# Selective attention and a gated convolution unit on one core: the last batch in two token parts, Q and K transposed by row halves, free bank pairs, and a new order

## The chip, the cores and the metric

The kernel runs on one core of a Trainium2 chip. The core has TensorE (PE, matrix products and transposes), VectorE (DVE), ScalarE (ACT), GpSimd (POOL) and SyncE (SP, which here only issues transfers), and 16 DMA engines that move data between memory and the on-chip buffer. Products of TensorE land in PSUM, eight banks of 512 float32 values on each of 128 partitions. The metric is the device time of one execution in microseconds (us). The profiled execution tells the span (first to last instruction) beside its own time.

## What is computed

Attention over 8 batches, 8 heads, 576 tokens, head width 64, with a bias from a running sum, then a gated unit over the joined heads (512 wide): a causal convolution with five taps gives a gate, one matrix a value, another the output.

```python
scores = scale * np.matmul(q, k.transpose(0, 1, 3, 2))
s_pos = np.maximum(s, 0.0)
cum = np.cumsum(s_pos, axis=-1)
bias = -(cum[:, :, :, None] - cum[:, :, None, :])
scores = np.where(causal, -1000000000.0, scores + np.minimum(bias, 0.0))
attn = softmax(scores)
x = matmul(attn, v), heads joined
for k in range(5):
    gate_pre += conv_w[k][None, None, :] * xp[:, k:k + S, :]
gate = 1.0 / (1.0 + np.exp(-gate_pre))
val = x @ w_val
out = gate * val @ w_out
```

## The kernel before

The work is cut into 32 units n, each a batch b = n // 4 and a pair of heads p = n % 4. One long list of steps, `ORDER`, was written by a planner. Each entry names a step, its indices, the engine that does it (S, G, T, A, V for SyncE, GpSimd, TensorE, ScalarE, VectorE) and where its result goes: a number of a PSUM bank, or of a buffer. The entries are emitted in that order, so each engine's queue is the list cut down to its own entries, and an engine works strictly in that order; waits between engines follow from the data.

The steps of a unit, with their lines:

- Loads `ld_q`, `ld_k` (L405, L410), tails of 64 tokens `ld_t` (L433), `ld_v` (L441 to L445); all on SyncE. Casts to bf16 `c_q`, `c_k` (the helper `copy`, L348, which is also the line of every evacuation).
- `qt` (L464): transposes of Q and K of the pair against an identity, eight of 128 x 128 into one bank; `qe` copies them to `QKT`. `tt`, `te` (L454): the tails in float32.
- `s0`, `s1`, `s2` (L475): three score steps of 512 columns for each head of the pair; the two heads lie in the upper and lower 64 rows of the operands, and write two neighbouring banks. `e0`, `e1`, `e2` (L523): exponentials of 2 x 512 into `P`. `s4`, `e4` (L500): the last 64 keys, for all four pairs at once after batch 0. The causal part is masked either with two further products (L486) or, for 16 units, on GpSimd (`mk`, L529).
- `vp` (L448): V scaled by the weights of the running sum, on GpSimd or VectorE. `av0`, `av` (L540): products of `P` and V for the two heads, 15 each, with a column of ones that gives the sum; `rec` (L545) and `nm` (L549) divide.
- `xt` (L562) transposes the result, `xe` copies it to `xT`; `t1` to `t4` (L584, L586 on VectorE, L588 on GpSimd) add the taps into `gp`; a tap on GpSimd needs a product `p2` to `p4` first (L573 on ScalarE, L575 on GpSimd). `th` (L598): tanh.
- `val` (L606): the value products, two halves of 288 tokens in two neighbouring banks; `glu` (L614) multiplies both halves with the gate. `out`, `outa` (L623): output products for 128 tokens; `oe` evacuates, `st` (L631) stores.
- `wu` (L556): products that nobody reads. `chk0`, `chk` (L634 to L641), `cnt`, `cntc` (L647, L656), `flag`: a test at the end that the reciprocals and the tap ratios lie in the range for which this path holds.

A pair of banks is always two neighbours:

```python
def pair(tok):
    j = at[tok][0]
    return bank[:, j:j + 2, :]
```

The list begins and ends thus:

```
ld_q.0.0:S wu.0:T:0 ld_s:S wu.1:T:7 ld_k.0.0:S wu.2:T:0 wu.3:T:7 ld_k.0.1:S wu.4:T:0 ld_t.0:S wu.5:T:7 wu.6:T:0
...
wu.19:T:7 ld_v.0.0:S wu.20:T:2 tt.0:T:0 qt.0.0.q:T:1 qt.0.0.k:T:2 qe.0.0.q:V cwT:T:3 qe.0.0.k:A wu.21:T:7 te.0:V
...
oe.3.8:V:2 st.3.4:S out.3.5:T outa.3.7:T:3 st.3.8:S oe.3.5:V:0 out.3.7:T outa.3.6:T:0 st.3.5:S oe.3.7:V:1 out.3.6:T
cnt:T:1 st.3.7:S oe.3.6:V:3 cntc:V st.3.6:S flag:S
```

Of the kernel before, what the change touches and what calls it, by code (L numbers as in the profile page):

```python
# [18 lines left out]
NKB = 5  # L19
# [152 lines left out]
WIN = [0, 128, 256, 384, 448]  # L172
BIG, TINY, FAR = 2.0 ** 100, -2.0 ** -70, -2.0 ** 27
# [4 lines left out]
ld_q.0.0:S wu.0:T:0 ld_s:S wu.1:T:7 ld_k.0.0:S wu.2:T:0 wu.3:T:7 ld_k.0.1:S wu.4:T:0 ld_t.0:S wu.5:T:7 wu.6:T:0  # L178
wu.7:T:7 ld_cw:S c_q.0.0:G wu.8:T:0 relu:V ld_q.0.2:S wu.9:T:7 scan:V wu.10:T:0 ld_q.0.1:S wu.11:T:7 wu.12:T:0
wu.13:T:7 ld_q.0.3:S wu.14:T:0 c_k.0.1:A wu.15:T:7 c_k.0.0:V wu.16:T:0 ld_k.0.2:S wu.17:T:7 centre:V wu.18:T:0  # L180
wu.19:T:7 ld_v.0.0:S wu.20:T:2 tt.0:T:0 qt.0.0.q:T:1 qt.0.0.k:T:2 qe.0.0.q:V cwT:T:3 qe.0.0.k:A wu.21:T:7 te.0:V
wu.22:T:6 ld_k.0.3:S s0.0:T:4:0 cwc:V s1.0:T:0 ld_v.0.1:S e0.0:A decT:T:2 qt.0.1.k:T:6 c_q.0.1:V wu.23:T:7 e1.0:A
qe.0.1.k:V mk.0:G qt.0.1.q:T:3 s2.0:T:4 qe.0.1.q:V wu.24:T:6 ld_q.1.0:S:0 e2.0:A wu.25:T:7 c_k.0.2:V c_q.0.3:G
s0.1:T:0:1 c_q.0.2:V qt.0.3.q:T:3 expw:A ld_k.1.0:S:2 s4.0.0:T:4 qe.0.3.q:V qt.0.2.q:T:6 vp.0.0:G e4.0.0:A
qt.0.2.k:T:7 e0.1:A qe.0.2.q:V s1.1:T:2 s4.0.1:T:4 qe.0.2.k:V ld_k.1.1:S wu.26:T:6 e1.1:A c_k.0.3:G av0.0:T:0 s2.1:T:6
e4.0.1:A ld_q.1.1:S s0.2:T:2:0 vp.0.1:V e2.1:A av.0:T s2.2:T:4 rec.0:V e0.2:A av0.1:T:6 ld_v.0.2:S nm.0:V av.1:T
c_q.1.0:G:0 e2.2:A qt.0.3.k:T:2 rec.1:V xt.0:T:3 qe.0.3.k:V mk.2:G qt.1.0:T:0 xe.0:A nm.1:V ld_v.0.3:S s1.2:T:4
qe.1.0:A wu.27:T:1 c_k.1.0:G:1 t1.0:V:0 xt.1:T:2 s0.3:T:6:1 e1.2:A xe.1:V s4.0.3:T:0 c_k.1.1:G t2.0:V ld_t.1:S e0.3:A
s4.0.2:T:4 t1.1:V:1 p2.1:G:0 e4.0.2:A ld_v.1.2:S t3.0:V e4.0.3:A s1.3:T:6 s2.3:T:4 e1.3:A c_q.1.1:G ld_v.1.4:S
# [8 lines left out]
c_q.2:G:0 ld_t.3:S xt.4:T:7 t1.5:V:0 val.1.1:T xe.4:A val.3.0:T:2 glu.1:V p3.5:A:1 val.3.1:T t1.4:V:2 p2.5:A:0
tt.2:T:4 t3.5:G s2.7:T:0 te.2:A glu.3:V qt.2.0:T:5 e2.7:A xt.6:T:6 t3.4:V val.0.0:T:2 p4.5:G:1 val.0.1:T qe.2.0:A
t2.4:V av0.7:T:0 t4.5:G qt.2.1:T:4 th.2:A:1 glu.0:V av.7:T qe.2.1:A xe.6:V val.2.0:T:2 rec.7:V t4.4:V c_k.2:G:0  # L200
val.2.1:T p2.6:A:1 s0.9:T:4:1 nm.7:V th.4:A:2 wu.32:T:7 glu.2:V s1.9:T:0 e0.9:A cast_wo:G xt.7:T:7 t1.6:V:2 qt.2.2:T:2
e1.9:A qt.2.3:T:3 t4.6:V s1.8:T:4 qe.2.2:A s0.8:T:0:0 t2.5:G xe.7:V out.0.2:T:6 t1.7:V:1 e0.8:A out.0.3:T:2 t2.6:G
t3.7:V qe.2.3:A out.0.1:T:0 t2.7:V oe.0.3:A:0 p3.6:G:0 out.0.0:T:1 oe.0.2:A:1 st.0.3:S oe.0.1:V:2 e1.8:A val.4.0:T:2
t4.7:V t3.6:G val.4.1:T oe.0.0:A:3 s0.10:T:6:2 th.7:A:1 glu.4:V st.0.0:S s4.2.3:T:0 s2.8:T:4 mk.8:G st.0.2:S e4.2.3:A
vp.2.0:V val.6.0:T:2 ld_v.3.4:S e2.8:A val.7.0:T:0 ld_t.4:S vp.2.2:G vp.2.1:V val.6.1:T th.6:A:2 val.7.1:T e0.10:A
ld_v.3.0:S c_k.3:G:0 av0.8:T:4 glu.6:V av.8:T ld_v.3.3:S glu.7:V th.5:A:0 s2.9:T:6 ld_v.3.1:S s2.10:T:2 rec.8:V e2.9:A
val.5.0:T:0 nm.8:V ld_v.3.2:S mk.10:G val.5.1:T e2.10:A st.0.1:S av0.9:T:6 glu.5:V ld_q.5:S:4 c_q.3:G:1 av.9:T
s1.10:T:2 rec.9:V tt.3:T:0 nm.9:V e1.10:A xt.8:T:1 s0.11:T:4:1 xe.8:V vp.2.3:G te.3:A s1.11:T:6 t1.8:V:0 av0.10:T:2
e0.11:A qt.3.1:T:0 p4.8:G:0 av.10:T p3.8:A:1 qe.3.1:V qt.3.0:T:4 e1.11:A out.0.7:T:5 t4.8:G rec.10:V qe.3.0:A nm.10:V
xt.9:T:0 xe.9:V xt.10:T:2 oe.0.7:A:1 t2.8:V s1.12:T:6 p4.9:G:0 xe.10:A s0.12:T:4:2 t1.9:V:2 out.0.6:T:3 e0.12:A t3.8:G  # L210
t1.10:V:1 out.0.8:T:1 e1.12:A oe.0.6:V:3 s2.11:T:4 mk.12:G oe.0.8:A:0 t3.9:V s2.12:T:6 st.0.6:S e2.11:A out.0.4:T:3
ld_k.5:S:0 t4.10:V t4.9:G qt.3.3:T:1 th.8:A:0 oe.0.4:V:2 av0.11:T:4 ld_q.4:S:3 qe.3.3:A t2.10:V vp.3.2:G tt.4:T:3
av.11:T e2.12:A te.4:V st.0.7:S qt.3.2:T:1 st.0.8:S rec.11:V vp.3.1:G t2.9:V out.0.5:T:3 qe.3.2:A nm.11:V th.9:A:1
vp.3.3:G s0.14:T:0:1 t3.10:V s0.13:T:6:0 e0.14:A s4.3.3:T:4 oe.0.5:V:3 xt.11:T:2 c_q.5:G:0 e4.3.3:A xe.11:V s2.13:T:0
# [57 lines left out]
def main_path(ctx, tc, q, k, v, s, moe_w_val, moe_conv_w, moe_w_out, out, okcnt):  # L272
# [469 lines left out]
```

## Time and profile before

| | us |
|---|---|
| three runs | 193.15, 196.77, 196.71 (median 196.71) |
| profiled execution | 193.35 |
| its span | 191.6 |

The profile's page gives the busy time of each engine. Its views used below: the waits (who waited for whom: total, times, longest), the timeline (start, duration, engine, line, operation), the chain of waits (which work, followed back from the last instruction, set the end), the groups (busy time and mean duration of like instructions, then the engine's idle time just before them and what ended it), the windows (busy time of PE, PEld, DVE, ACT, POOL in a stretch, then the granted TensorE clock as a share of full speed, the DMA share and GB/s). A group's mean duration counts the overlap of pipelined instructions; busy time divided by their number does not.

### The profile page before, as it was taken

What the parts mean: (1) busy time and instruction counts of PE and PEld (TensorE: products, weight loads), DVE (VectorE), ACT (ScalarE), POOL (GpSimd) and SP (SyncE); (2) the same over time, 40 slices, a digit from 0 to 9 for tenths busy, and PEclk for the clock granted to TensorE, in tenths of its full rate; (3) what the DMA queues carried; (4) which work ended last, traced back from release to release, by engine and by line L of the source; (5) the groups of instructions that cost most, each with busy time, mean ns of one, the idle gap of its engine ahead of it and who ended that gap; (6) DMA issues with size and microseconds to landing.
All of it is one profiled execution on the core that took longest, in us unless ns stands there. A gap on an engine that the chain in (4) does not pass through costs nothing.

```text
span 191.6 us, 6160 instructions
## 1 busy us (share of the span) xinstructions
PE 176.6 (92%) x2481; PEld 119.3 (62%) x2481; DVE 172.9 (90%) x279; ACT 166.2 (87%) x214; POOL 166.8 (87%) x136
## 2 busy tenths in 40 slices
PE   6999796899998999999997899999999999989991
PEld 2457483578556846677755577675756764757740
DVE  5597999889989799998999999999999899999973
ACT  2179999979999699989899989999999999898930
POOL 6036989998999989999999999999999999998910
PEclk9999999699999999999999999999999999999999
DMA  5998999999999997999999999279550005200515
GB/s 149 269 258 305 255 185 288 317 335 239 238 298 292 192 260 285 307 399 189 194 192 314 363 344 216 107 249 254 139 159 29 29 5 201 76 2 3 221 74 207
DMA packets 62281, 40.43 MB, mean 211 GB/s; under 512 B 47333, under 2 KB 49381, under 8 KB 62250
## 3 DMA queue, kind: packets, MB, share of 16 engines
q1 hardware_dynamic: 62250, 40.01, 76.9%
q8 instruction: 20, 0.33, 0.7%
q14 instruction: 11, 0.09, 0.2%
HBM read 30.57 MB, written 9.44 MB: 209 GB/s over the span
## 4 chain that ended last, share of the span: by engine, by line
PE 33%; DVE 21%; ACT 21%; POOL 10%; issue 9%; DMA 3%; SPq 1%; DVEq 0%; ACTq 0%; POOLq 0%
ACT P L523 9%; PE bank L540 9%; PE bank L623 6%; POOL gp L588 5%; PE bank L475 5%; PE bank L606 5%; DVE gp L586 4%; PE bank L464 3%; DVE xn L549 3%; ACT QKT L348 3%; DVE QKT L348 3%; DVE glu L614 3%; ACT th L598 3%; DMA tail<-in_k_dram 3%; POOL pr L575 2%
## 5 line engine op out<-in xcount | busy, mean ns | idle before, releaser
L523 ACT ACTIVATE P<-bank 128x1024 bf16<-128x1024 f32 x96 | 94.5, 1039 | 4.0 <-PE bank L475 2.4
L588 POOL TENSOR_TENSOR gp<-gp,pr 128x572 f32<-128x572 f32 (+2 forms) x38 | 56.2, 1486 | 3.7 <-ACT pr L573 0.9
L586 DVE SCALAR_TENSOR_TENSOR gp<-bank,cwr,gp 128x574 f32<-128x574 bf16 (+2 forms) x58 | 46.1, 802 | 0.6
L475 PE MATMUL bank<-QKT 64*128 64x128 bf16 (+4 forms) x576 | 38.0, 241 | 5.1 <-ACT P L523 2.8
L606 PE MATMUL bank<-xT,wv 128*128 128x288 bf16 x256 | 36.1, 286 | 2.1 <-DVE xT L348 0.6
L540 PE MATMUL bank<-Vp,P 128*128 128x65 bf16 x960 | 35.9, 194 | 0.7 <-ACT P L523 0.5
L540 PEld LDWEIGHTS <-P 128*128 128x128 bf16 x960 | 33.4, 98 | 4.6 <-issue 2.5
L623 PE MATMUL bank<-wo,glu 128*128 128x512 bf16 x144 | 35.3, 380 | 0.1
L575 POOL TENSOR_TENSOR pr<-xT,cwr 128x572 f32<-128x572 bf16 (+2 forms) x28 | 32.7, 1175 | 1.4 <-DVE xT L348 0.8
L475 PEld LDWEIGHTS <-QKT 64*128 64x128 bf16 x576 | 18.5, 94 | 21.8 <-issue 14.8
L606 PEld LDWEIGHTS <-wv 128*128 128x128 bf16 x256 | 23.8, 97 | 10.7 <-issue 3.4
L448 POOL TENSOR_TENSOR Vp<-vst,w 128x650 bf16<-128x650 f32 x22 | 29.0, 1335 | 0.5 <-ACT w L369 0.5
L598 ACT ACTIVATE th<-gp,cwr 128x576 f32<-128x576 f32 (+1 forms) x33 | 25.2, 780 | 3.1 <-POOL gp L588 1.9
L584 DVE SCALAR_TENSOR_TENSOR gp<-xT,cwr,bank 128x576 f32<-128x576 bf16 x32 | 25.7, 809 | 1.3 <-ACT xT L348 0.2
L549 DVE TENSOR_TENSOR xn<-bank,recs 128x640 bf16<-128x640 f32 x32 | 26.0, 819 | 0.6
L348 ACT COPY QKT<-bank 128x1024 bf16<-128x1024 bf16 (+1 forms) x25 | 24.9, 1014 | 1.8 <-PE bank L464 1.8
L614 DVE SCALAR_TENSOR_TENSOR glu<-th,bank 128x576 bf16<-128x576 f32 (+1 forms) x33 | 23.9, 731 | 2.5 <-ACT th L598 1.1
L529 POOL TENSOR_SCALAR_AFFINE_SELECT P<-P 128x1024 bf16<-128x1024 bf16 x16 | 17.5, 1094 | 8.8 <-ACT P L523 8.8
L623 PEld LDWEIGHTS <-glu 128*128 128x128 bf16 x144 | 12.5, 97 | 14.0 <-issue 2.3
L464 PE MATMUL bank<-ident,qkb 128*128 128x128 bf16 x256 | 19.3, 219 | 0.3 <-DVE gp L586 0.3
L464 PEld LDWEIGHTS <-qkb 128*128 128x128 bf16 x256 | 15.4, 98 | 3.5 <-issue 1.6
L348 POOL CAST qkb<-first 128x2048 bf16<-128x2048 f32 (+2 forms) x11 | 15.5, 1410 | 0.8 <-DMA first<-in_k_dram 0.4
(61 smaller groups left out, 182.7 us busy)
## 6 DMA issues: line engine op xcount, KB each, us to landing
out_dram<-ot SPq DMA_DIRECT2D x36, 256.0 KB, 3.1
vst<-in_v_dram SPq DMA_DIRECT2D x28, 256.0 KB, 5.8
first<-in_q_dram SPq DMA_DIRECT2D x7, 512.0 KB, 7.3
first<-in_k_dram SPq DMA_DIRECT2D x7, 512.0 KB, 8.2
qkf<-in_q_dram SPq DMA_DIRECT2D x5, 512.0 KB, 6.2
qkf<-in_k_dram SPq DMA_DIRECT2D x5, 512.0 KB, 6.5
vst<-in_v_dram SPq DMA_DIRECT2D x15, 128.0 KB, 4.6
first<-in_q_dram SPq DMA_DIRECT2D x6, 256.0 KB, 4.6
```

The source lines that it names most:

```text
L348: (act.copy if e is act else e.tensor_copy)(dst, src)
L464: pe.transpose(bank16[:, at["qt", b, p, *w][0], c * 512 + j * 128:c * 512 + (j + 1) * 128], qk_src(which, b, p, j if w else 4 * c + j), ident)
L475: pe.matmul(ps[:, hh, c0:c0 + nq], QKTs[b % 2][r, 1, p, k0:k0 + 128], QKTs[b % 2][r, 0, p, q0:q0 + nq], **kw)
L523: act.activation(out=Pt(n)[:, :, step * 512:(step + 1) * 512], in_=pair((f"s{step}", n)), func=AF.Exp, scale=0.125)
L540: pe.matmul(ps[:, qb * 65:qb * 65 + 65], lhsT, Vps[b % 2][:, kb, 2 * p + hh, :], start=(kb == 0), stop=(kb == qb))
L549: vec.tensor_tensor(xns[b % 2][:, :, p * 128:(p + 1) * 128].rearrange("t g (w d) -> t w g d", w=2), pair(("av", n))[:, :, 0:325].rearrange ...
L575: pool.tensor_tensor(pr, xTs[b % 2][:, c, 4:4 + S - m], r.to_broadcast([128, S - m]), ALU.mult)
L586: vec.scalar_tensor_tensor(gp[:, m:S], xps(n)[:, 0:S - m], r, gp[:, m:S], ALU.mult, ALU.add)
L588: pool.tensor_tensor(gp[:, m:S], gp[:, m:S], prs[at[f"p{m}", n][0]][:, m:S], ALU.add)
L598: act.activation(out=thof(n)[:, r], in_=gps[at["t1", n][0]].rearrange("p (h s) -> p h s", h=2)[:, r], func=AF.Tanh, scale=cwr[:, n % 4, 4:5])
L606: pe.matmul(ps, wv[:, dc, c * 128:(c + 1) * 128], xTs[b % 2][:, dc, 4 + o:4 + o + 288], start=(dc == 0), stop=(dc == 3))
L623: pe.matmul(bank_of(u, i), glu2[:, c, i * 128:i * 128 + 128], wo[:, c, :], start=(c == 0), stop=(c == 3))
```

## The change

- The units of the last batch (28 to 31) run in two token parts of 384 and 192 tokens. Their three score steps and exponentials of 2 x 512 become four of 2 x 384 (`u0` to `u3`, `f0` to `f3`), the mask has two steps (`mk`, `ml`), and `av`, `rec`, `nm`, `xt`, `xe`, the taps, their products, `th`, `val` and `glu` each come once for a part.
- From batch 1 on, the transposes of Q and K of two pairs are one step `qq`: each 128 x 128 transpose becomes two, of the upper and lower 64 rows, into two banks; `qe` reads both banks.
- A pair of banks may be any two.
- `glu` runs once for each half of the value products, everywhere, and each half has a bank of its own.
- The test at the end takes a minimum and a sum of the reciprocals instead of two compares for each.
- `ORDER` is new. In it six of batch 0's loads are issued by ScalarE; the casts of batch 1's Q and batch 2's K are on ScalarE; all 32 `vp` are on GpSimd (22 before); ScalarE has 28 output evacuations and VectorE 8 (20 and 16 before); GpSimd masks 15 whole units and four parts of units 28, 30 and 31 (16 whole units before); there are 40 unread products (33 before), eleven of them together behind unit 5's second score step (`s1.5`); two output blocks rather than five are held back for the last tanh; the last batch's parts are interleaved.

```diff
+HALF_STEPS = [
+    [(0, 0, 128, 0), (1, 128, 128, 128), (2, 256, 128, 256)],
+    [(0, 128, 256, 0), (1, 256, 128, 256)],
+    [(3, 384, 128, 0), (3, 512, 64, 128), (0, 384, 192, 192)],
+    [(1, 384, 192, 0), (2, 384, 192, 192)],
+]
+PARTS = [(0, 384, (0, 1, 2)), (384, 576, (3, 4))]
...
+ld_k.0.0:A ld_q.0.0:S ld_k.0.1:A wu.0:T:0 ld_t.0:S wu.1:T:7 wu.2:T:0 wu.3:T:7 ld_q.0.1:S wu.4:T:0 ld_k.0.2:A ld_s:S
+wu.5:T:7 ld_q.0.2:A wu.6:T:0 ld_v.0.0:S ld_k.0.3:A wu.7:T:7 c_k.0.0:V ld_q.0.3:A qt.0.0.k:T:0 wu.8:T:2 c_q.0.0:V
+qe.0.0.k:A qt.0.0.q:T:1 ld_v.0.1:S wu.9:T:7 c_k.0.1:V qe.0.0.q:A wu.10:T:2 qt.0.1.k:T:0 s0.0:T:1+2:0 qe.0.1.k:V
+wu.11:T:7 e0.0:A tt.0:T:3 ld_k.1.0:S:2 wu.12:T:0 te.0:V wu.13:T:7 wu.14:T:0 c_q.0.1:G wu.15:T:7 s2.0:T:3+1 ld_k.1.1:S
...
+t4.31.1:G glu.29.1:V out.3.5:T:0 st.3.6:S th.30.1:A:1 glu.28.1:V st.3.4:S t2.31.1:V glu.30.1:V val.31.1:T:7
+th.31.1:A:2 outa.3.8:T:2 oe.3.5:A:2 glu.31.1:V chk:V out.3.8:T st.3.5:S outa.3.7:T:0 oe.3.8:A:3 out.3.7:T st.3.8:S
+cnt:T:2 oe.3.7:A:1 cntc:V st.3.7:S flag:S
...
+        if ("qq", b, p // 2) in at:
+            copy(e, QKTs[b % 2][:, :, p, 0:512].rearrange("d w (r x j) -> d w r x j", r=2, j=8),
+                 both_rows(b, p).rearrange("d r (j x w) -> d w r x j", w=2, j=8))
+            return
...
-    def pair(tok):
-        j = at[tok][0]
-        return bank[:, j:j + 2, :]
+    def both(two):
+        lo, hi = two
+        return bank[:, lo:hi + 1:hi - lo, :]
...
+    def half_T(out, src, r):
+        return pe.transpose(out, src[64 * r:64 * r + 64, :], ident[64 * r:64 * r + 64, 64 * r:64 * r + 64])
+
+    def both_rows(b, p):
+        lo, hi = sorted(at["qq", b, p // 2])
+        return bank16[:, lo:hi + 1:hi - lo, p % 2 * 512:p % 2 * 512 + 512]
+
+    def qk_T2(e, b, h):
+        for p in range(2):
+            for j in range(8):
+                for r in range(2):
+                    half_T(both_rows(b, 2 * h + p)[:, r, j * 64:j * 64 + 64], qk_src(None, b, 2 * h + p, j), r)
...
-    def within(e, o, rf):
-        e.tensor_scalar(o, rf, 5e-35, None, ALU.is_ge)
-        e.scalar_tensor_tensor(o, rf, 1.5e31, o, ALU.is_le, ALU.mult)
+    def extremes(e, i, rf):
+        e.tensor_reduce(stat[:, i:i + 1], rf, AX.X, ALU.min)
+        e.tensor_reduce(stat[:, 2 + i:3 + i], rf, AX.X, ALU.add)
```

More of the change, by code (lines that the diff above doesn't have):

```diff
@@ L198 @@
[L198 to L202, printed above, removed]
@@ L329, in main_path @@
     cw = ots[3][0:5]
-    cwT = one.tile([128, 4, 5], FP32, name="cwT")
     cwr = one.tile([128, 4, 5], FP32, name="cwr")
@@ L404, in f @@
             if b == 0:
-                sync.dma_start(out=first[part][which],
+                e.dma_start(out=first[part][which],
                                in_=(q, k)[which][0, HP[part], 0:512, :].rearrange("h (p j) d -> p h (j d)", j=4))
@@ L565, in x_evac @@
+    def both_rows(b, p):
[4 more added lines that the diff above has]
+            for j in range(8):
+                for r in range(2):
+                    half_T(both_rows(b, 2 * h + p)[:, r, j * 64:j * 64 + 64], qk_src(None, b, 2 * h + p, j), r)
+    def x_evac(e, n, *h):
         b, p = divmod(n, 4)
-        copy(e, xTs[b % 2][:, p, 4:4 + S], xps(n))
+        lo, hi = span(*h)
+        copy(e, xTs[b % 2][:, p, 4 + lo:4 + hi], xps(n, *h)[:, lo:hi])
@@ L594, in tanh @@
     def tanh(e, n, *hf):
+        if split(n):
+            lo, hi = span(*hf)
+            act.activation(out=ths[at["th", n, *hf][0]][:, lo:hi], in_=gps[at["t1", n, *hf][0]][:, lo:hi],
+                           func=AF.Tanh, scale=cwr[:, n % 4, 4:5])
+            return
         if hf:
```

405 lines of the change are left out of this document (236 added, 169 removed).

## The prediction

> **What bounds the kernel now.** I read the page first, then ScalarE's waits, then its start and its end.
>
> ```profile
> span 191.6 us, 6160 instructions
> ...
> PE 176.6 (92%) x2481; PEld 119.3 (62%) x2481; DVE 172.9 (90%) x279; ACT 166.2 (87%) x214; POOL 166.8 (87%) x136
> ```
>
> Four engines are within 11 us of each other, so none alone is the bound: a gain needs a shorter start, a shorter end, fewer waits, or less work on all four. The change moves work onto ScalarE, so I balance that engine's time. Who kept it waiting:
>
> ```profile
> ACT qkb L348 <- DMA first<-in_k_dram: 5.4, 1, 5.4
> ACT P L523 <- PE bank L475: 2.4, 3, 1.6
> ACT th L598 <- POOL gp L588: 1.9, 4, 0.7
> ACT QKT L348 <- PE bank L464: 1.8, 1, 1.8
> ACT ot L348 <- PE bank L623: 1.5, 3, 0.7
> ACT P L523 <- PE bank L486: 1.1, 2, 1.0
> ACT th L598 <- DVE ok L634: 1.0, 1, 1.0
> ```
>
> Its start in the timeline, and the chain of waits there:
>
> ```profile
> 0.82 1.28 ACT L348 ACT_TABLE_LOAD   x1 [0.82 <-PEq L726]
> 7.54 0.62 ACT L348 CAST qkb<-first 128x512 bf16<-128x512 f32 x1 [5.44 <-DMA first<-in_k_dram]
> 9.97 0.59 ACT L348 COPY QKT<-bank 128x512 bf16<-128x512 bf16 x1 [1.81 <-PE bank L464]
> 11.18 1.02 ACT L523 ACTIVATE P<-bank 128x1024 bf16<-128x1024 f32 x1 [0.62 <-PE bank L475]
> ```
> ```profile
> 0.82 0.46 SPq L405
> ...
> 3.76 4.96 DMA tail<-in_k_dram
> ...
> 8.86 0.63 PE bank L454 x4
> ```
>
> The first exponential starts at 11.18, because TensorE's queue has the tails' transposes (L454) ahead of the first Q, K transposes, and the tail lands at 8.7. The end (ScalarE, chain, VectorE):
>
> ```profile
> 182.88 0.96 ACT L598 ACTIVATE th<-gp,cwr 128x288 f32<-128x288 f32 x2 [0.96 <-DVE ok L634]
> ```
> ```profile
> 182.77 4.62 PE bank L623 x20
> ```
> ```profile
> 187.46 0.69 DVE L348 COPY ot<-bank 128x512 f32<-128x512 f32 x1 [0.23 <-PE bank L623]
> ```
>
> After the last tanh (183.84) come 7.76 us in which five output blocks are made one after another. From the first exponential to that point are 172.66 us, of which ScalarE works 166.2 less 1.28, 0.62, 0.59 (before) and 0.6 (one evacuation after) = 163.1, and idles 9.5. So the span is 11.2 + 163.1 + 9.5 + 7.8 = 191.6, and the profiled run took 193.35, 1.75 more. Of the runs one stands there (193.15); the median, 196.71, is 3.4 higher. I forecast a run like the profiled one.
>
> **Work on ScalarE.** Rows (engine, busy, mean):
>
> ```profile
> L523 ACT ACTIVATE P<-bank 128x1024 bf16<-128x1024 f32 x96 | 94.5, 1039 | 4.0 <-PE bank L475 2.4 <-PE bank L486 1.1
> ...
> L348 ACT COPY QKT<-bank 128x1024 bf16<-128x1024 bf16 x24 | 24.3, 1031 | 0.0
> L598 ACT ACTIVATE th<-gp,cwr 128x576 f32<-128x576 f32 x31 | 24.3, 796 | 2.1 <-POOL gp L588 1.9 <-DVE glu L614 0.2
> ...
> L348 ACT COPY ot<-bank 128x512 f32<-128x512 f32 x20 | 12.0, 606 | 1.5 <-PE bank L623 1.5
> ...
> L348 ACT COPY xT<-bank 128x576 bf16<-128x576 bf16 x11 | 7.1, 650 | 0.6 <-PE bank L562 0.5
> ...
> L500 ACT ACTIVATE P<-bank 128x512 bf16<-128x512 f32 x7 | 4.4, 627 | 0.0
> ...
> L573 ACT ACTIVATE pr<-bank,cwr 128x573 f32<-128x573 bf16 x5 | 3.7, 744 | 0.1
> ```
>
> Busy per instruction: exponential 0.98 at 1,024 wide, 0.63 at 512, so 0.81 at 768. The last batch's 12 become 16 of 768: 16 x 0.81 - 12 x 0.98 = +1.1. Tanh: 0.78 whole, 0.48 at half, so about 0.61 and 0.45 for 384 and 192 tokens; 28 + 4 pairs against 31 + 2 halves: +1.0. Output evacuations 20 to 28: +4.8. Casts: two of 1,024 (1.0 each, as the QKT copy) and one of 2,048 (1.7, on the same slope) for the one of 0.62: +3.1. QKT copies: one whole less (-1.0), two of 512 more (+1.2). X evacuations: six whole fewer, six parts at about 0.4: -1.4. Tap products: two whole fewer, one part: -1.1. Sum +7.7. Two evacuations follow the last tanh rather than one, so 163.1 + 7.7 - 0.6 = **170.2** lie before it.
>
> **The other engines.**
>
> ```profile
> L448 POOL TENSOR_TENSOR Vp<-vst,w 128x650 bf16<-128x650 f32 x22 | 29.0, 1335 | 0.5 <-ACT w L369 0.5
> ...
> L614 DVE SCALAR_TENSOR_TENSOR glu<-th,bank 128x576 bf16<-128x576 f32 x31 | 23.0, 749 | 2.1 <-ACT th L598 0.8 <-PE bank L606 0.5 <-ACT ot L348 0.4
> ...
> L448 DVE TENSOR_TENSOR Vp<-vst,w 128x650 bf16<-128x650 f32 x10 | 12.2, 1232 | 0.0
> L556 PE MATMUL bank<-ident 128*128 128x512 bf16 x33 | 12.0, 492 | 1.6 <-POOL ident masks.py:199 1.4 <-DVE QKT L348 0.2
> ...
> L348 DVE COPY ot<-bank 128x512 f32<-128x512 f32 x16 | 11.0, 686 | 1.2 <-PE bank L623 1.1
> ...
> L614 DVE SCALAR_TENSOR_TENSOR glu<-th,bank 128x288 bf16<-128x288 f32 x2 | 0.9, 454 | 0.3 <-ACT th L598 0.3
> ```
> ```profile
> L588 POOL TENSOR_TENSOR gp<-gp,pr 128x572 f32<-128x572 f32 (+2 forms) x38 | 56.2, 1486 | 3.7 <-ACT pr L573 0.9 <-DVE recs L545 0.9 <-DVE gp L586 0.3
> ```
>
> VectorE: value products by halves make 64 of 0.45 from 31 of 0.74 and two halves, +4.9; ten V scalings go, -12.2; eight output evacuations go, -5.5. Whole taps go from 90 to 84 and 18 parts come, priced like the gate's wholes and halves of the same shape: 18 x 0.45 - 6 x 0.74 = +3.7; parts of normalising and the rest about +3. Sum -6. GpSimd: ten V scalings at 1.32 come, +13.2; its additions go from 38 wholes to 28 and 10 parts of about 0.8, -14.9 + 8; products likewise some -3; masks and casts -0.8. Sum +2.5. The scalings stand in its queue ahead of masks and taps, and the tanh that waits for the taps (1.9 above) can wait longer. Both stay below ScalarE, which becomes the longest.
>
> A copy out of two banks at once is new for Q, K. I price it as before, since the exponentials read two banks at 0.98 for 1,024 elements, no more than the copy of 1,024 from one bank (24.3/24 = 1.01); if it cost a tenth more, ScalarE would have 2.4 more. The bank pair that an exponential reads need no longer be neighbours: the same price, and the same doubt with it.
>
> TensorE: 224 whole transposes become 448 of half the rows and half the width. Whole ones and the nearest row of 64 wide products from half the rows:
>
> ```profile
> 89.91 1.51 PE L464 MATMUL bank<-ident,qkb 128*128 128x128 bf16 x24
> ```
> ```profile
> 151.10 0.29 PE L475 MATMUL bank<-QKT 64*128 64x64 bf16 x8
> ```
>
> A whole one takes (1.51 - 0.22)/23 = 0.056, a 64 wide one (0.29 - 0.19)/7 = 0.014, since the two row halves run at once. So two pairs cost 32 x 0.014 = 0.45 instead of 16 x 0.056 = 0.90; times 14, -6.3, or nothing if the halves run in turn (32 x 0.027 is about 0.9). I take -5 for the turns between shapes. Seven more unread products at 0.36 add 2.5. Here the Trainium skill speaks against the change: TensorE: Matmul & The Clock Gate (Wait — 56ns, not 53.3ns?) says that products never start less than about 25 ns apart, which would leave 0.8 of 0.9. The row above, at 14 ns, disagrees for products from different row halves. The page TensorEngine Tiling (Array Packing), Key Properties, adds that a change of tiling mode drains the array; no row shows a price for it.
>
> **Start.** K of pair 0 is now the first load on ScalarE's queue, beside Q on SP's, and the tails' transposes come after the first scores. Loads into this tile:
>
> ```profile
> DMA to landing us min/median/max: 3.0/5.0/9.2
> ```
>
> Issued at 0.8 plus 3.0 to 5.0 (the table load may go first and take 1.3 of it): landed at 3.8 to 5.8, say 4.5. Then a cast 0.6, transposes 0.4, two evacuations of 0.6, scores 0.7: the first exponential at about **7.5** (6.8 to 8.8). The tail comes behind two or three loads, some 8 plus transpose, evacuation and scores: 9.8, so the second exponential waits 1.4. ScalarE's six issues, some 0.46 to 0.6 each, lie in the time in which it waited 5.4 for data; SP's queue loses them, so the V loads behind them are issued earlier, and all loads share what was a transfer of about 5 us each: if the first two come no sooner for it (5.0 rather than 3.0), the first exponential stands at 8.8 and 1.3 is lost.
>
> **End.** Only two blocks hang on the last tanh: gate product 0.45, five products at 4.62/20 (1.2), evacuation 0.6, store and close as before (191.6 - 188.15 = 3.45): **5.7**. The shorter closing test takes the 0.96 before the last tanh away.
>
> **Waits.** TensorE ran at half clock and ScalarE waited for it:
>
> ```profile
> 35.00:36.00 1.00, 1.00 (x6) 0.13 (x4) 1.00 (x2) 1.00 (x2) 1.00 (x2) 0.50 1.06 397
> ```
> ```profile
> 39.49 1.02 ACT L523 ACTIVATE P<-bank 128x1024 bf16<-128x1024 f32 x1 [0.96 <-PE bank L486]
> ```
>
> The unread products now stand just there, so of the 9.5 this 0.96 goes, and the closing test's 0.96. Waits for TensorE's products (1.8 + 0.9 + 0.1) I halve, as TensorE gets shorter, GpSimd's 1.9 and the other 2.9 too, since all three now run ahead of ScalarE: 1.4 + 0.95 + 1.45, and 1.4 for the tail: **5.2** (1.4 to 9.0). Any two banks making a pair costs nothing itself; it can only shift these waits.
>
> Sum: 7.5 + 170.2 + 5.2 + 5.7 + 1.75 = **190.4** (1.5% under 193.35; 3.2% under the median).
>
> **Rivals.** *ScalarE is kept full* (0.27): three engines with slack and free choice of banks leave only the tail's 1.4: 186.6. For it: the last batch's parts feed ScalarE to the end. Against: before, no engine did better than 95% in its dense stretch.
>
> *The halves don't overlap* (0.15): TensorE, with its unread products, gets longer and none of the waits on it or its followers falls: 9.0, so 194.2. For it: no transposes by halves in this trace; against: the 0.014 above.
>
> *ScalarE blocked by loads* (0.16): batch 1's Q casts and batch 2's K cast now stand in ScalarE's queue, ahead of all its exponentials of that batch; behind them wait the scores' banks, so TensorE too. By my count it reaches the first at 26, when those loads, issued at about 20, land (25 to 29). A landing of 9.2 instead of 5.0 at both places costs 8.4: 198.8. It decides from 3 us in all. Against: after the start no engine waited for a load.
>
> The forecast's case has 0.42, its own range 188 to 192.5. Range 185.5 to 196. About 2% is what a measurement can tell from no change: faster than 189.5 are the first rival and half of the forecast's case, 0.48; slower than 197.2 most of the last, 0.13; 0.39 between.
>
> **What would show it.** First exponential at 7 to 8 and a gap before the second; ScalarE busy about 174, VectorE 167, GpSimd 169; 32 half transposes of a step in some 0.65; clock 1.00 throughout; 5.7 us behind the last tanh. It is wrong if ScalarE's idle time between is outside 1.4 to 9, or if its casts wait for loads.

## The result, and the profile after

| | before | after |
|---|---|---|
| runs, us | 193.15, 193.51, 196.71, 196.77 (median 195.11) | 312.90, 314.60, 314.82, 319.55 (median 314.71) |
| ratio to before, 95% interval | 1 | 1.626 (1.615 to 1.637) |
| profiled execution and its span, us | 193.35, 191.6 | 319.55, 317.7 |
| mean granted TensorE clock in it | 0.989 | 0.822 |

The change made the kernel 63% slower. Medians take all runs, ratios only those in a kernel's faster state, and the profiled execution of after is a slower one (319.55). The page after, its head and the row of the clock:

```profile
span 317.7 us, 6693 instructions
...
PE 220.1 (69%) x2716; PEld 136.6 (43%) x2734; DVE 167.7 (53%) x320; ACT 181.0 (57%) x231; POOL 165.9 (52%) x148
...
PEclk9779675699699975657995999977699855997699
```

The work is near what was forecast for VectorE (167) and GpSimd (169), and 7 us more than forecast for ScalarE (174); no engine is busy for more than 69% of the span. So the time went into waiting, on all engines and from one end to the other. TensorE now stands idle again and again, and its granted clock is below 1 in most slices. Who waited for whom (total, times, longest):

```profile
PE bank L518 <- ACT P L569: 18.1, 24, 1.2
...
ACT P L569 <- DVE xn L626: 12.6, 9, 1.7
DVE recs L620 <- ACT P L569: 12.0, 7, 3.0
DVE gp L684 <- ACT P L569: 11.0, 6, 3.9
ACT P L569 <- PE bank L518: 10.8, 14, 1.6
ACT P L569 <- PE bank L607: 10.7, 7, 2.8
```

Three of these rows name two instructions of which neither hands data to the other. An exponential (L569) reads scores and writes `P`; the normalising step (L626) reads a product of `P` and V and writes `xn`. Nothing goes straight from the one into the other, and yet exponentials wait for it, 12.6 us in all; the reciprocals (L620) and the taps on VectorE (L684) wait for exponentials. In the waits before, none of the three pairs of lines stands at all.

One place shows how it works. The list there reads, with banks behind the engine's letter:

```
av0.4:T:3+6 av.4:T rec.4:V e0.5:A vp.1.3:G av0.6:T:0+2 nm.4:V av.6:T e1.5:A s2.5:T:1+5 rec.6:V vp.1.1:G xt.4:T:3 nm.6:V e2.5:A
```

`e0.5`, `e1.5` and `e2.5` read banks 1 and 5, 4 and 7, 1 and 5; `nm.4` reads 3 and 6, `nm.6` reads 0 and 2. The timeline of after, ScalarE and then VectorE:

```profile
63.71 1.02 ACT L569 ACTIVATE P<-bank 128x1024 bf16<-128x1024 f32 x1 [3.50 <-DVE recs L620]
65.68 1.02 ACT L569 ACTIVATE P<-bank 128x1024 bf16<-128x1024 f32 x1 [0.95 <-DVE xn L626]
68.27 1.02 ACT L569 ACTIVATE P<-bank 128x1024 bf16<-128x1024 f32 x1 [1.56 <-DVE xn L626]
```
```profile
64.76 0.82 DVE L626 TENSOR_TENSOR xn<-bank,recs 128x640 bf16<-128x640 f32 x1 [1.15 <-ACT P L569]
67.10 0.22 DVE L620 RECIPROCAL recs<-bank 128x10 f32<-128x10 f32 x1 [1.51 <-PE bank L518]
67.35 0.82 DVE L626 TENSOR_TENSOR xn<-bank,recs 128x640 bf16<-128x640 f32 x1
```

The two engines take turns: `nm.4` starts when `e0.5` ends (63.71 + 1.02 = 64.73), `e1.5` when `nm.4` ends (64.76 + 0.82 = 65.58), `e2.5` when `nm.6` ends (68.17). The banks say why. Bank 6 of `nm.4` lies between 4 and 7, bank 2 of `nm.6` between 1 and 5, and bank 3 of `nm.4` between 1 and 5. Each instruction that takes two distant banks waits as if it took all the banks between them too.

The start and the end of after, by the same view of ScalarE:

```profile
13.76 1.02 ACT L569 ACTIVATE P<-bank 128x1024 bf16<-128x1024 f32 x1 [5.09 <-PE bank L531]
...
311.46 0.46 ACT L698 ACTIVATE th<-gp,cwr 128x192 f32<-128x192 f32 x1 [0.68 <-DVE gp L684]
```

The first exponential ran at 7.65, as forecast. The second, at 13.76, reads banks 1 and 3, and its row names a product of another step (L531) in bank 2. Little of the 5.09 is due to that. The scores that it reads began only at 13.16, since TensorE had first waited 2.50 for the tail:

```profile
13.16 0.53 PE L518 MATMUL bank<-QKT 64*128 64x320 bf16 x6
```

In the run e1 below, which has no distant pairs, the same scores begin at 10.96 and the exponential 0.44 later; here it is 0.60. Behind the last tanh (311.92) stand 5.8 us, where 5.7 were forecast.

### The profile page after: what moved, and what is told of

Same layout as the page of the kernel before. It is cut to its first block, busy times and chain, and to the rows that moved or that the text cites. A ratio compares the mean times of both kernels' runs of the same rounds, so it can differ in the third digit from the quotient of the medians.

```text
span 317.7 us, 6693 instructions
## 1 busy us (share of the span) xinstructions
PE 220.1 (69%) x2716; PEld 136.6 (43%) x2734; DVE 167.7 (53%) x320; ACT 181.0 (57%) x231; POOL 165.9 (52%) x148
## 4 chain that ended last, share of the span: by engine, by line
PE 42%; ACT 28%; DVE 15%; issue 7%; POOL 4%; DMA 3%; SPq 0%; ACTq 0%; DVEq 0%; POOLq 0%
ACT P L569 17%; PE bank L717 9%; PE bank L607 9%; PE bank L518 8%; DVE xn L626 6%; ACT QKT L374 6%; PE bank L737 6%; PE bank L633 3%; ACT P L583 3%; DMA tail<-in_k_dram 3%; PE bank L639 3%; PE bank L642 2%; POOL qkb L374 2%; DVE QKT L374 2%; DVE gp L679 2%
## 5 line engine op out<-in xcount | busy, mean ns | idle before, releaser
L569 ACT ACTIVATE P<-bank 128x1024 bf16<-128x1024 f32 x84 | 84.5, 1023 | 80.8 <-DVE xn L626 12.6
L687 POOL TENSOR_TENSOR gp<-gp,pr 128x572 f32<-128x572 f32 (+6 forms) x38 | 47.3, 1247 | 58.5 <-DVE gp L684 28.3
L684 DVE SCALAR_TENSOR_TENSOR gp<-bank,cwr,gp 128x574 f32<-128x574 bf16 (+5 forms) x70 | 50.9, 739 | 18.8 <-ACT P L569 11.0
L717 PE MATMUL bank<-xT,wv 128*128 128x288 bf16 (+2 forms) x256 | 46.4, 324 | 13.6 <-ACT P L569 7.8
L607 PEld LDWEIGHTS <-P 128*128 128x128 bf16 x960 | 40.2, 108 | 22.4 <-issue 17.1
L668 POOL TENSOR_TENSOR pr<-xT,cwr 128x572 f32<-128x572 bf16 (+6 forms) x29 | 29.1, 1008 | 30.0 <-DVE xT L374 26.5
L592 POOL TENSOR_SCALAR_AFFINE_SELECT P<-P 128x1024 bf16<-128x1024 bf16 (+2 forms) x19 | 20.0, 1054 | 35.8 <-ACT P L569 32.0
L726 DVE SCALAR_TENSOR_TENSOR glu<-th,bank 128x288 bf16<-128x288 f32 (+2 forms) x64 | 27.4, 446 | 18.8 <-PE bank L717 5.5
L626 DVE TENSOR_TENSOR xn<-bank,recs 128x640 bf16<-128x640 f32 (+2 forms) x36 | 26.8, 746 | 18.0 <-ACT P L569 4.6
L679 DVE SCALAR_TENSOR_TENSOR gp<-xT,cwr,bank 128x576 f32<-128x576 bf16 (+2 forms) x36 | 26.6, 742 | 9.2 <-ACT P L569 7.3
L620 DVE RECIPROCAL recs<-bank 128x10 f32<-128x10 f32 (+2 forms) x36 | 7.5, 210 | 40.1 <-ACT P L569 12.0
L639 PE MATMUL bank<-ident,xn 128*128 128x128 bf16 x164 | 18.4, 253 | 9.5 <-DVE xn L626 4.5
L704 ACT ACTIVATE th<-gp,cwr 128x576 f32<-128x576 f32 x28 | 21.3, 772 | 0.0
```

What stands on the lines that cost most here:

```text
L569: act.activation(out=Pt(n)[:, :, step * 512:(step + 1) * 512], in_=pair((f"s{step}", n)), func=AF.Exp, scale=0.125)
L607: pe.matmul(ps[:, o:o + 65], lhsT, Vps[b % 2][:, kb, 2 * p + w, :], start=(kb == 0), stop=(kb == qb))
L626: vec.tensor_tensor(xns[b % 2][:, g, p * 128:(p + 1) * 128].rearrange("t g (w d) -> t w g d", w=2), ps[:, :, :, 0:64], recs[:, n, :, g].un ...
L668: pool.tensor_tensor(pr, xTs[b % 2][:, c, 4 + lo - m:4 + hi - m], r.to_broadcast([128, hi - lo]), ALU.mult)
L679: vec.scalar_tensor_tensor(gp[:, lo:hi], xT[:, 3 + lo:3 + hi], r, xps(n, *h)[:, lo:hi], ALU.mult, ALU.add)
L684: vec.scalar_tensor_tensor(gp[:, lo:hi], xps(n, *h)[:, lo - m:hi - m], r, gp[:, lo:hi], ALU.mult, ALU.add)
```

## The experiments

The first theory (A) is the one just read from the trace: the new line `bank[:, lo:hi + 1:hi - lo, :]` touches two banks, but the layer that records the instructions and puts in the waits takes it for the whole range from `lo` to `hi`. Waits would then follow not from the data alone, as the part on the kernel before has it, but from all the banks that an instruction is taken to touch. In after's list 153 steps have a pair of banks; in 128 the two aren't neighbours, and 337 banks lie in between. In the programs as built, a wait can be held against the banks and buffers of its two instructions: among TensorE, VectorE and ScalarE, 10 of 695 waits before join instructions that share none (all ten are those of a weight load, whose product does share one), and 355 of 759 after. The rivals of e1 to e3 put the cause elsewhere in the change.

Medians stand beside those of before on the same chip, since chips differ (193.1 to 195.5 for before):

| run | time, us | before, us | ratio (95%) | busy PE, DVE, ACT, POOL, us | clock |
|---|---|---|---|---|---|
| e1 neighbours | 200.99 | 195.03 | 1.029 (1.017 to 1.040) | 177.1, 164.4, 172.4, 165.2 | 0.972 |
| e2 before, far pairs | 378.11 | 195.03 | one run | 248.6, 178.5, 177.3, 164.1 | 0.740 |
| e3 renumbered | 255.58 | 195.03 | one run | 194.5, 165.4, 177.8, 165.7 | 0.916 |
| e4 e1 without 11 unread products | 199.75 | 195.53 | 1.025 (1.016 to 1.034) | 172.8, 164.8, 172.3, 165.3 | 0.972 |
| e5 e1 with whole transposes | 199.24 | 195.53 | 1.019 (1.007 to 1.032) | 176.4, 164.6, 172.6, 165.4 | 0.991 |
| e6 e1, first loads on SyncE | 199.26 | 195.53 | 1.019 (1.009 to 1.029) | 176.6, 164.2, 172.3, 164.0 | 0.966 |
| e7 before, value by halves | 194.37 | 195.53 | 0.994 (0.988 to 1.000) | 176.3, 175.0, 166.8, 166.5 | 0.991 |
| e8 e5, 8 evacuations on VectorE | 200.07 | 193.13 | 1.037 (1.031 to 1.043) | 180.4, 167.7, 169.2, 165.5 | 0.967 |
| e9 before, early start | 193.63 | 193.13 | 1.003 (0.999 to 1.007) | 174.8, 172.7, 166.5, 167.0 | 0.991 |
| e10 before, short test | 192.70 | 193.13 | one run | 173.7, 173.3, 166.5, 166.0 | 0.997 |
| e11 e5, e6, e8 together | 199.29 | 193.13 | 1.033 (1.026 to 1.039) | 177.7, 167.8, 169.3, 164.2 | 0.981 |
| e12 before, row halves | 209.22 | 194.79 | 1.080 (1.073 to 1.087) | 178.3, 176.1, 168.4, 167.2 | 0.973 |
| e13 before, e12's banks | 204.13 | 194.79 | 1.056 (1.050 to 1.061) | 177.3, 176.7, 168.3, 166.8 | 1.000 |

**e1: neighbours only.** After, with its order and its engines, but every pair of banks dealt anew as two neighbours; single banks are dealt anew with them:

```diff
-av0.4:T:3+6 av0.6:T:0+2 s2.5:T:1+5
+av0.4:T:6+7 av0.6:T:4+5 s2.5:T:0+1
```

> The changed kernel with every step in its place; only the bank numbers are dealt anew, so that each pair is two neighbours again. Theory A (an instruction that touches banks a and b also waits for whoever uses the banks between them): the waits between ScalarE, VectorE and TensorE on banks that they do not share are gone, ScalarE idles 5 to 10 us between its first exponential and the last tanh, 187 to 195 us. Rival B (the new order itself keeps the engines waiting): 300 us or more. Rival C (TensorE falls to half clock from the turns between whole and half transposes): 300 us or more, with the half transposes slow.

Measured: 200.99. Of the 120 us that after lost, 114 are gone (314.71 to 200.99), though on other chips. The rivals, which left the time near after's, are out; A's own range, 187 to 195, was too low by 6, and its 5 to 10 us of idle time by 7 (17.1). The place shown above, in e1's timeline:

```profile
46.67 2.85 ACT L569 ACTIVATE P<-bank 128x1024 bf16<-128x1024 f32 x3 [2.97 <-PE bank L607]
```
```profile
46.97 0.82 DVE L626 TENSOR_TENSOR xn<-bank,recs 128x640 bf16<-128x640 f32 x1
47.71 0.21 DVE L620 RECIPROCAL recs<-bank 128x10 f32<-128x10 f32 x1
47.95 0.82 DVE L626 TENSOR_TENSOR xn<-bank,recs 128x640 bf16<-128x640 f32 x1
```

The three exponentials now run in one block of 2.85 us, and VectorE normalises beside them; in after they took from 63.71 to 69.29. In e1's waits no exponential waits for `xn`.

**e2: the same fault put into before.** Before, with its own order, engines and work. The bank numbers are renamed so that each of its 171 pairs lies four banks apart:

```diff
+        if e == "T" and slots:
+            slots[0] = slots[0] // 2 + 4 * (slots[0] % 2)
-        return bank[:, j:j + 2, :]
+        return bank[:, j:j + 5:4, :]
```

> The kernel before with its plan untouched; only banks are renumbered so that the two banks of each pair lie four apart (0 and 4, 1 and 5, ...). Theory A: some 480 waits on banks in between, where the changed kernel has some 355, so 270 to 360 us, with ScalarE and VectorE waiting for each other. Rivals B and C: 193 to 197 us, since order and transposes are those of before.

Measured: 378.11, nearly twice before, past A's 360, with nothing of the change in it but the distant pairs. The foreign wait comes with them:

```profile
ACT P L523 <- DVE xn L549: 24.6, 13, 3.8
```

**e3: fewer banks between.** After, with only the names of its eight banks permuted (0, 1, ..., 7 become 0, 4, 1, 7, 2, 5, 6, 3). Which step shares which bank with which stays as it was; 83 pairs remain distant, with 188 banks between them instead of 337.

> The changed kernel with its plan and its pairs untouched; the eight banks are renumbered (0,4,1,7,2,5,6,3) so that fewer lie between two of a pair: 188 instead of 337 in all. Theory A: some 200 waits on banks in between instead of 355, so about 260 us (225 to 290). Rivals B and C: 310 to 320 us, since nothing else differs.

Measured: 255.58, where A said about 260. A permutation of names changes nothing but what lies between, so time follows that: 337 in between 315, 188 some 256, none (e1, where the numbers are dealt anew) 201. The waits by program fall in step: 355, 199 and 6 that share no bank or buffer (482 of 712 in e2). A is settled.

What is open after e1 is smaller: 2 to 3% above before, where the forecast was 2 to 3% below. The next runs take the other terms of the sum one at a time.

**e4: without the unread products.** e1 without the eleven behind `s1.5` (`wu.29` to `wu.39` left out of the list).

> e1_neighbours without its eleven unread products wu.29 to wu.39 that stand together behind s1.5. Theory A1 (what e1 lacks against the forecast is partly TensorE's queue: the eleven, 4.28 us at 41.40 in e1's timeline, hold the value products of unit 4, for which VectorE then waits 5.9 and ScalarE about 3): 196.5 to 199 us beside e1's 201, the waits of VectorE's reciprocals for the bank of the value products at 42 to 48 shrink from 5.9 to under 3. Rival (TensorE would stand there anyway, waiting for the V scalings of batch 1 that GpSimd ends only at about 46): 200 to 202, the wait moves to the V scalings. Second rival (the unread products keep the clock up, as they are meant to): above 202, with a lower granted clock behind 41 us.

Measured: 199.75, 0.3% nearer to before than e1, within the intervals, and between the range of A1 and that of the first rival. VectorE's wait at that place, in e1 and in e4, fell from 5.90 to 4.67, not to under 3:

```profile
46.71 0.22 DVE L620 RECIPROCAL recs<-bank 128x10 f32<-128x10 f32 x1 [5.90 <-PE bank L607]
```
```profile
44.45 0.22 DVE L619 RECIPROCAL recs<-bank 128x10 f32<-128x10 f32 x1 [4.67 <-PE bank L606]
```

The 60 products of `P` and V that follow, in e1 and in e4:

```profile
41.40 4.28 PE L633 MATMUL bank<-ident 128*128 128x512 bf16 x11
...
45.51 1.99 PE L607 MATMUL bank<-Vp,P 128*128 128x65 bf16 x60
```
```profile
42.54 3.46 PE L606 MATMUL bank<-Vp,P 128*128 128x65 bf16 x60 [1.72 <-ACT P L568]
```

Without the eleven, these products start 2.97 us earlier (TensorE then waits 1.72 for an exponential) and take 1.47 longer, at a lower clock (0.69 in the 10 us from 40, where e1 has 0.75). So both A1 and the second rival are half right in the mechanism, and neither in the time: the unread products take TensorE's time and the products behind them are faster for it, which gives back about half (1.47 of 2.97).

**e5: whole transposes.** e1 with each `qq` undone into two `qt` of eight 128 x 128 transposes, one bank each.

> e1_neighbours with the row halves undone: each qq becomes two qt steps of eight whole 128 x 128 transposes, one bank each. By the prediction's term (-5 us of TensorE's time for the halves): TensorE's busy time goes from e1's 177 to 181 to 184, and the time, since TensorE is again the longest engine by 8, from 201 to 202.5 to 205. Rival (the halves run one after the other, or their turns of shape cost what they save): TensorE's busy time within 1.5 of e1's, the time within 2 of it.

Measured: 199.24, not above e1's 200.99, so the price expected is not there; the rival's numbers hold (busy 176.4 against 177.1). Yet the transposes themselves are as much shorter as forecast. One step of e1 (two pairs) and the same of e5:

```profile
56.12 0.64 PE L642 MATMUL bank<-ident,qkb 64*128 64x64 bf16 x32
```
```profile
49.92 1.07 PE L504 MATMUL bank<-ident,qkb 128*128 128x128 bf16 x16
```

14 x (1.07 - 0.64) = 6.0 us. The row of e1 gives (0.64 - 0.19)/31 = 0.0145 us from one half transpose to the next, 0.19 being the duration of one alone. The Trainium skill, TensorE: Matmul & The Clock Gate (Wait — 56ns, not 53.3ns?), has 25 ns as the least; the trace disagrees for products from two row halves. What of the 6.0 was given back the rows show in part: e1 ran at a clock of 0.90 from 10 to 60 us, e5 at 1.00, and its eleven unread products took 4.28 where e5's took 2.90 (1.66 and 1.24).

**e6: who issues the first loads.** e1 with all of batch 0's first loads issued by SyncE (six `:A` become `:S`).

> e1_neighbours with all of batch 0's first loads issued by SyncE, in the order of the list. Theory A2 (the early start is bounded by what the DMA engines move, not by which engine issues): the first exponential moves from 8.04 by less than 1 us, the time is 200 to 202. Rival, the prediction's own step (the issue on ScalarE's idle queue brings the first exponential forward, since SyncE's issues take about 0.5 to 0.6 each): the first exponential at 9.5 to 11, the time 202 to 204.

Measured: 199.26; the first two exponentials:

```profile
7.81 1.02 ACT L569 ACTIVATE P<-bank 128x1024 bf16<-128x1024 f32 x1 [1.74 <-PE bank L518]
9.86 1.02 ACT L569 ACTIVATE P<-bank 128x1024 bf16<-128x1024 f32 x1 [1.02 <-PE bank L518]
```

The first is where e1 had it (8.04), the second 1.54 earlier (11.40 in e1), since TensorE starts on the tail at 7.94 rather than 9.48. The rival expected 9.5 to 11 for the first, and 202 to 204; A2's 200 to 202 is just missed. The early start comes from the order of the loads, not from a second engine that issues them. The Trainium skill says the same in DMA: Bandwidth & Descriptors (Issuing engines are not separate DMA queues): transfers of all issuing engines share the same 16 DMA engines, and a second issuer saves only the time of issuing. The trace agrees (7.81 with one issuer, 8.04 with two).

**e7: value products by halves in before.** 64 half `glu` for the 31 whole and two halves.

> Before with its 31 whole products of value and gate each done as two halves, as after has it, nothing else changed. The prediction's price: VectorE +4.9 us busy (172.9 to 177.8). VectorE is within 7 us of the longest engine: if its work is nowhere on the path that sets the end, 194 to 196 (before 195); if it is all on it, 199 to 200. Theory: in between, 196 to 198.

Measured: 194.37, within 1% of before: the case in which the work is nowhere on the path. The theory, 196 to 198, misses. VectorE's busy time rose by 2.1 (172.9 to 175.0), not 4.9; the 64 halves are busy for 25.7 us, 0.40 each, where the prediction took 0.45 from two of them.

**e8: ScalarE's added work given back.** e5 with eight output evacuations on VectorE (`oe.1.0:A:2` becomes `oe.1.0:V:2`, and so on).

> e5_whole_transposes with eight of ScalarE's output evacuations (oe.0.5, oe.1.0, oe.1.2, oe.1.6, oe.1.7, oe.1.8, oe.2.0, oe.2.1) on VectorE, at the same places of the order, as many as before had there. ScalarE's busy time falls by about 4.8 (172.6 to 168), VectorE's rises by 5.5 (164.6 to 170). Theory (what the neighbour pairs leave over before is mostly work moved onto ScalarE, which is on the path): 196 to 198 beside e5's 199.2. Rival (the engines wait for one another in this order, whoever has the work): 198.5 to 201.

Measured: 200.07; ScalarE's busy time fell by 3.4, and the time didn't. The theory falls, the rival holds: in this order, less work on ScalarE did not make the time shorter.

**e9: the early start alone.** Before with `ld_k.0.0` second and the tails behind the first scores:

```diff
-... tt.0:T:0 qt.0.0.q:T:1 qt.0.0.k:T:2 ... te.0:V ... s0.0:T:4:0 ... e0.0:A
+... qt.0.0.q:T:1 qt.0.0.k:T:2 ... s0.0:T:4:0 ... e0.0:A ... tt.0:T:0 ... te.0:V
```

> Before with its first steps in another order: K of pair 0 is the second load on SyncE's queue, the first Q, K transposes, scores and exponential stand ahead of the tails' transposes, as in after; nothing else changed. First exponential at 7 to 8 instead of 11.2 in both cases. Prediction's step (what the first exponential comes earlier, less a wait of 1.4 for the tail, is kept to the end): 192 to 193.5 beside before's 195.5. Rival, theory A2 (the loads of the next pairs land no sooner, so ScalarE waits for them and has done by 22 us what it had done before): 194.5 to 196.

Measured: 193.63 beside 193.13. ScalarE in e9, and one row of before:

```profile
7.65 1.02 ACT L523 ACTIVATE P<-bank 128x1024 bf16<-128x1024 f32 x1 [1.21 <-PE bank L475]
...
11.04 1.02 ACT L523 ACTIVATE P<-bank 128x1024 bf16<-128x1024 f32 x1 [1.85 <-PE bank L475]
...
16.53 2.85 ACT L523 ACTIVATE P<-bank 128x1024 bf16<-128x1024 f32 x3
```
```profile
17.00 2.85 ACT L523 ACTIVATE P<-bank 128x1024 bf16<-128x1024 f32 x3
```

The first exponential is 3.53 earlier (11.18 before), the sixth to eighth only 0.47, and at the end (spans 191.8 and 191.6) nothing is left. The ratio, 1.003, is where the rival had it (194.5 to 196 beside 195.5), but not quite for its reason. The second exponential reads scores that need the tail, and the tail's transposes (L454) start at 8.95, no earlier than before (8.86). ScalarE had one exponential early and then waited for the tail; behind it the steps of the next pairs follow in TensorE's queue.

**e10: the shorter closing test alone.** Before with `within` replaced by `extremes`.

> Before with the test at the end done with a minimum and a sum, as after has it. Prediction's step (the wait of 0.96 before the last tanh was for the test on VectorE): that wait goes. Rival (it was for the last tap on GpSimd, which ended at 181.45 + 1.40 = 182.85 in before's trace, 0.03 before the tanh began; the row named the engine wrongly): 0.8 to 1.1 stays. The time within 1 us of before in both cases.

Measured in the trace: the wait stays, and its row now has another name. The last tanh in e10, and the last tap of before:

```profile
182.14 0.96 ACT L599 ACTIVATE th<-gp,cwr 128x288 f32<-128x288 f32 x2 [0.95 <-POOL gp L589]
```
```profile
181.45 1.40 POOL L588 TENSOR_TENSOR gp<-gp,pr 128x573 f32<-128x573 f32 x1 [0.33 <-DVE gp L586]
```

In before the tap ended at 182.85 and the tanh began at 182.88; the test's first step (L634) ended at 182.63 + 0.26 = 182.89, no sooner, and yet the row gave its name to the wait.

**e11: the parts together.** e5 with e6's loads and e8's evacuations.

> After's plan with neighbour pairs, whole transposes, the eight evacuations on VectorE, and all first loads on SyncE (e5, e6 and e8 together). Theory: the parts add up, 195 to 198, at best even with before. Rival (each part only moves a wait): 198.5 to 201.

Measured: 199.29, 3.3% above before: the rival. Parts that moved nothing alone moved nothing together. No version with after's list beats before.

**e12 and e13: row halves alone, and their banks.** Before with `qk_T` and `qk_evac` by row halves from batch 1 on, into two neighbouring banks; the bank numbers of the list dealt anew (e12). The same numbers with whole transposes, the second bank left empty (e13).

```diff
+        if not w:
+            for j in range(8):
+                for r in range(2):
+                    half_T(both_rows(b, p)[:, r, j * 64:j * 64 + 64], qk_src(None, b, p, j), r)
+            return
```

> Before with one part of the change alone: from batch 1 on the transposes of Q and K are done by row halves, into two neighbouring banks, one pair at a time; the bank numbers of the list are dealt anew for it, nothing else changed. Prediction's term: TensorE's busy time -5 us (176.6 to about 171.5) at a full clock, and since TensorE is the longest engine by 4, the time falls by 2 to 4 beside e13. Rival (TensorE waits for the others at those places, so shorter transposes only lengthen its waits, and its clock falls with its load): TensorE's busy time falls by less than 3, the time within 1 us of e13's.

> Control for e12: before with whole transposes, but with the bank numbers of e12, which leave a second bank empty at each transpose. Theory: the dealing alone costs 0 to 2 us, so 193 to 197 beside before's 193 to 196. Rival (bank dealing sets the waits of these kernels, and is what e1 lacks against the forecast): 197 or more.

Measured: 209.22 and 204.13. In e13 its rival holds (197 or more): its fastest run, 202.41, is above the slowest of before there, 198.20. In e12 neither time holds, since it is 5 us above e13, but the rival was right that TensorE's busy time would not fall. The groups of transposes, e12 and e13 (busy, mean ns, then idle before them):

```profile
L462 PE MATMUL bank<-ident,qkb 64*128 64x64 bf16 x448 | 11.9, 192 | 5.0 <-ACT P L539 3.3 <-DVE QKT L348 0.7 <-DVE xn L565 0.7
...
L476 PE MATMUL bank<-ident,qkb 128*128 128x128 bf16 x32 | 2.8, 220 | 0.0
```
```profile
L464 PE MATMUL bank<-ident,qkb 128*128 128x128 bf16 x256 | 19.6, 219 | 2.5 <-ACT P L523 1.9 <-DVE xn L549 0.3 <-ACT QKT L348 0.2
```

The group is shorter by 19.6 - 11.9 - 2.8 = 4.9 us, the term that the prediction had. TensorE's busy time is not (178.3 against 177.3, at a clock of 0.973 against 1.000), it stands idle 2.5 us more ahead of its transposes, which now need two free banks at once, and the time is 5 us longer; what makes up the other half of the 5 is not shown. And e13 has the work, the order and the neighbours of before; only the numbers of its banks differ, and it is 5.6% slower, with TensorE idle for 200.7 - 177.3 = 23.4 us of the span (before 191.6 - 176.6 = 15.0). No bank lies between here: all that new numbers change is which earlier step must have left a bank before the next one writes it.

## Why the prediction was wrong

**The step that failed** is the last sentence of its part on waits: "Any two banks making a pair costs nothing itself; it can only shift these waits." It costs the waits of all the banks in between. The access itself is no dearer (an exponential takes 1,023 ns on average in after and 1,039 before); the waiting is. By the balance of the prediction, after's ScalarE starts its exponentials at 7.65, ends its last tanh at 311.92, and works some 177 us in between (181.0 less the table load, two copies before and three after); so it idles about 127 us, where the forecast had 5.2 and no more than 9.0. The miss is made of 127 - 5 in waits, and of 7 of work more than forecast, since instructions of ScalarE that run one at a time don't overlap with their neighbours (three exponentials in a block take 2.85, alone 3 x 1.02). Of the 122 in waits, 110 go when the pairs are neighbours (e1 idles 17.1); the other 12 are the matter of the next part. The diff had the cause in sight: a slice with a step, and a list in which 128 of 153 pairs are distant. No rival asked what the recording layer makes of a slice with a step.

**Without those waits (e1)** the sum can be checked term by term. First exponential 8.04 (forecast 7.5), work between 168.3 (170.2), idle 17.1 (5.2), end 5.85 (5.7): 199.3, and 201.08 with what lies around the span. Work and end were nearly right, the idle time was short by 12. Two of its terms are shown to be wrong, one bought nothing where it was tried, and one wait was left out:

- The early start was expected to be kept but for a wait of 1.4 us for the tail. That wait was 2.33 in e1, and e9 keeps none of 3.53.
- The closing test's 0.96 was a misnamed wait for GpSimd's tap (e10).
- TensorE's 5 us were in the transposes (4.9 in e12, 6.0 in e5) but not in its busy time, and not in the time. Waits for its products, to be halved, grew instead. ScalarE's waits in e1 (before had 2.4 in the row that answers to the first):

```profile
ACT P L569 <- PE bank L518: 6.9, 8, 2.3
...
ACT P L569 <- PE bank L607: 3.6, 3, 3.0
```

- The new step `qq` puts two pairs into the same two banks, each in its own half of them. In five of the 14 steps the two copies out of the banks (`qe`) are on different engines, and there one waits for the other, though neither needs the other's values: 3.8 us in e1 on ScalarE, where before and e5 have no such row. Without it (e5) the time is within e1's interval.

```profile
ACT QKT L374 <- DVE QKT L374: 3.8, 4, 1.4
```

Where e1 falls behind is seen in the windows from 10 to 60 us, of e1 and of before (busy time of PE, PEld, DVE, ACT, POOL, then the clock):

```profile
10.00:60.00 50.00, 42.07 (x674) 27.00 (x674) 37.96 (x66) 40.96 (x51) 39.84 (x32) 0.90 1.01 255
```
```profile
10.00:60.00 50.00, 46.24 (x711) 32.15 (x710) 46.23 (x72) 47.50 (x64) 43.39 (x34) 0.97 1.06 270
```

ScalarE does 6.5 us less in that stretch, VectorE 8.3 less. Which wait starts it, the order or the new dealing of banks, stays open: e13 shows that a dealing alone can cost more than the 3% in question, and e4, e5, e6, e8 and e11 each moved e1 by no more than its interval.

**The rest.** The price of halves for value and gate was too high (2.1 for 4.9, e7). No cast waited for a later batch's loads, so that rival did not come about. A clock of 1.00 throughout was wrong for after (0.822) and, from 10 to 60 us, for e1. The mode-change drain that the prediction cited has no row of its own in any run.

## What to carry to other kernels

Before an access with a step through banks or tiles is priced at nothing, ask what the recording layer takes it to touch: if it takes the range, each instruction waits for strangers, and in a kernel whose engines are all near full such waits multiply. A wait between two instructions that share no data is the sign of it, and a list with the names of the banks permuted is a cheap test. A bank's number is a resource of its own: here, shorter work that needs two free banks at once made the kernel 5 us slower, and a start that ran ahead of its data gained nothing.

## What the runs showed of the hardware that was not expected

- The clock was lower where TensorE stood idle for longer, and the same work then kept it busy for longer. With after's list it idled 22 us of the span in e1 (clock 0.972), 59 in e3 (0.916) and 98 in after (0.822), and was busy for 177, 194.5 and 220. With before's list it idled 15 us in before (0.989) and 128 in e2 (0.740), and was busy for 177 and 249. The order is not strict: e13 idled 23 us at 1.000. The products of 288 columns took 286 ns on average before and 329 in after:

```profile
L606 PE MATMUL bank<-xT,wv 128*128 128x288 bf16 x256 | 36.1, 286 | 2.1 <-DVE xT L348 0.6 <-ACT P L523 0.5 <-DVE gp L586 0.3
```
```profile
L717 PE MATMUL bank<-xT,wv 128*128 128x288 bf16 x224 | 41.5, 329 | 13.6 <-ACT P L569 7.8 <-ACT P L583 2.5 <-DVE xn L626 1.2
```

- Half transposes of the two row halves follow one another every 0.0145 us, whole ones every (1.07 - 0.22)/15 = 0.057 us, so two halves cost half of a whole one; and that saving was nowhere in TensorE's total. By an estimate it was there at full clock: busy time times clock is 172.1 in e1 against 174.8 in e5, and 173.5 in e12 against 177.3 in e13. The runs with halves had the lower clock, and by this estimate it took the saving back.
